# A single scale factor of one weight's conversion read from a tile, which a ScalarE result must precede

## The chip, the cores and the metric

The kernel runs on one core of a Trainium2 chip. The metric is the device time of one execution in microseconds (us). Three runs of the kernel before took 575.41, 574.70 and 574.67 us; the median is 574.7 us.

## What is computed

A chain of three parts in float32, in which every part reads the output of the one ahead of it:

```python
state = gamma * state + outer(k[t], v[t]); y[t] = scale * q[t] @ state   # 2 x 8 heads, 768 steps, 64 wide
x  = y as (1536 tokens, 512)
xn = x / rms(x) * rms_g                                                   # first feed-forward part
x  = (silu(xn @ w_gate) * (xn @ w_val)) @ w_out                           # 512 -> 1536 -> 512
h  = x @ w_in                                                             # second feed-forward part
out = maximum(0.01 * h, h) @ w2_out                                       # 512 -> 2048 -> 512
```

The weights arrive as 64-bit floats. The kernel turns them into 32-bit floats on the chip.

## The kernel before, in words

**Tiles.** The 1536 tokens are three blocks of 512. A weight is cut into tiles of 128 by 512, named by kind and number: g, v and o (gate, value and output of the first feed-forward part, 12 of each) and i and p (input and output of the second one, 16 of each). So i1 is the second of the i-weights and o11 the last of the o-weights.

**Conversion of one weight.** One DMA brings the 64-bit words of a tile to `raw_i1` (three such buffers, `RAWS`). ScalarE (ACT) makes three passes over it in `prepare`: L608 the high words into `wa_i1` (four buffers), L609 the low words, scaled by 2 to the -29, into `wb_i1` (two buffers, tag "b" of the pool `stage`), and L613 the signs into half of `wb_i1`. L609 and L613 together are called the low passes here. VectorE (DVE) then clamps and shifts (`wa_i1` at L534 and L539) and adds `wb_i1` to it (L553), after which `wa_i1` is the 32-bit weight and the `wb` buffer is free for the weight two further on. For TensorE (PE) the weight is split into a high part (ACT, L556) and a low part (DVE, L560), called `w_i1`; a product of weight and input is three matmuls, high by high, low by high and high by low.

**Sums of weights.** Two of three token blocks are computed with seven half products in place of eight (the scheme of Strassen and Winograd, `quad` for g, v and i, `seventh` for o and p). This needs, for each pair of weights, two more tiles: `w_si2` and `w_si3` for the pair i2, i3. DVE makes four half-width sums in place (L490), and again ACT writes the high part (L493) and DVE the low part (L497).

**A pair of i-weights on PE** (L1110, `quad`): seven groups of six matmuls into three PSUM banks X, Y and Z. With the pair i0, i1: X by `w_i0`, Y by `w_i0`, then on with X by `w_si0` (group p6 in the code), with Z by `w_si1` (p5), X by `w_si1` (p7), Z by `w_si0` (p3) and X by `w_i1` (p4). Between two uses of X or Z the sum so far has to be copied out: by ACT at L1127 (`is1`, `is5`, `iu2`) or by DVE with an addition at L1136. ACT then applies the leaky maximum at L1046. The other products of the first block (L657, `i0_0` and so on) and the products with o or p (L908, L775, L692) fill the time between.

**What sets the order.** The first stretch is a list written by hand (`ORDER`). From there a planner (`run`) emits the operations step by step, and the scheduler of the tile framework moves them: it lists each engine's instructions in the order in which, by its own estimate, they can start. Each engine then runs its own list strictly in order. So an added dependence changes the lists of all engines behind it.

Of the kernel before, what the change touches and what calls it, by code (L numbers as in the profile page):

```python
# [8 lines left out]
F32 = mybir.dt.float32  # L9
F32R = mybir.dt.float32r  # L10
I32 = mybir.dt.int32
U32 = mybir.dt.uint32
F16 = mybir.dt.float16
AF = mybir.ActivationFunctionType
ALU = mybir.AluOpType
AX = mybir.AxisListType

P = 128
# [3 lines left out]
G1 = [4, 4, 4]  # L22
# [44 lines left out]
def chain_kernel(ctx: ExitStack, tc: tile.TileContext, qk_t, kv, w1, w2, mask, qdec, kdec, sdec, rms_g, ident, out):  # L67
    nc = tc.nc
# [16 lines left out]
    gp = ctx.enter_context(tc.tile_pool(name="gp", bufs=3))  # L85
    scr = ctx.enter_context(tc.tile_pool(name="scr", bufs=SCRATCH))
    ps_acc = ctx.enter_context(tc.tile_pool(name="ps_acc", bufs=1, space=bass.MemoryType.PSUM))
    dram = ctx.enter_context(tc.tile_pool(name="dram", bufs=1, space=bass.MemoryType.DRAM))
    attn_pools = ctx.enter_context(ExitStack())
    score_pool = ctx.enter_context(ExitStack())  # L90
# [2 lines left out]
    at = attn_pools.enter_context(tc.tile_pool(name="at", bufs=4))  # L93
    sm = attn_pools.enter_context(tc.tile_pool(name="sm", bufs=4))

    held = [dram.tile([P, 512], F32, name=f"held{i}") for i in range(4)]
    mask_sb = const.tile([P, 2, NPAIR, CH], F32, name="mask_sb")
    qdec_sb = const.tile([P, NPAIR, CH], F32, name="qdec_sb")
# [305 lines left out]
        )  # L404

    wt = {}
    slots = [[units, UNITS, set()]]
    groups = [list(range(sum(g[:i]), sum(g[:i + 1]))) for g in (G1, G2) for i in range(len(g))]
    groups = [("gvo" if i < len(G1) else "ip", fs) for i, fs in enumerate(groups)]

# [34 lines left out]
    def free(*keys):  # L445
        for s in slots:
            s[2].difference_update(keys)


    def fetch():  # L450
        if fetched[0] < min(len(sources), taken[0] + RAWS):
            key, src = sources[fetched[0]]
            fetched[0] += 1
            raw[key] = raws.tile([P, 512, 2], I32, tag="raw", name=f"raw_{key}")
            cut = 512 if key in IN_HALVES else 1024
            for n in range(0, 1024, cut):
                nc.sync.dma_start(
                    out=raw[key].rearrange("p n two -> p (n two)")[:, n:n + cut], in_=src.bitcast(I32)[:, n:n + cut]
                )
# [3 lines left out]
    def open_unit():  # L463
        if started[0] == len(wq):
            return None
        key, src = wq[started[0]]
        v = nc.vector

        def room(key):
            slot = next((s for s in slots if len(s[2]) < s[1]), None)  # L470
            if slot is not None:
                slot[2].add(key)
            return slot

        after = next((k for k, x in wq[started[0] + 1:] if x is not None), None)
        if src is None:
            n, f = key[1], int(key[2:])

            names = (key, f"s{n}{f + 1}")
            places = [room(k) for k in names]  # L480
            if None in places:
                free(*names)
                return None
            started[0] += 1
            a, e = kept.pop(f"{n}{f}"), kept.pop(f"{n}{f + 1}")
            a_one, a_two, e_one, e_two = a[:, :2 * P], a[:, 2 * P:], e[:, :2 * P], e[:, 2 * P:]
            us = [s[0].tile([P, 2, 512], F32R, tag="u", name=f"w_{k}") for s, k in zip(places, names)]

            def combine(out, in0, in1, op):
                return lambda: v.tensor_tensor(out=out, in0=in0, in1=in1, op=op)  # L490

            def high_part(u, x):
                return lambda: nc.scalar.activation(out=u[:, 0, :], in_=x, func=AF.Copy)  # L493

            def low_part(u, x, k):
                def put():
                    v.tensor_tensor(out=u[:, 1, :], in0=x, in1=u[:, 0, :].bitcast(F32), op=ALU.subtract)  # L497
                    wt[k] = u

                return put  # L500

            if n in "op":
                return key, None, {
                    "1": combine(e_two, a_two, e_two, ALU.add),
                    "2": combine(a_two, a_one, a_two, ALU.subtract),
                    "3": combine(a_one, e_two, a_one, ALU.subtract),
                    "H": high_part(us[0], a),
                    "4": combine(e_one, e_one, a_one, ALU.subtract),
                    "h": high_part(us[1], e),
                    "L": low_part(us[0], a, names[0]),  # L510
                    "l": low_part(us[1], e, names[1]),
                }
            return key, None, {
                "1": combine(e_two, e_one, e_two, ALU.add),
                "2": combine(e_one, a_one, e_one, ALU.subtract),
                "3": combine(a_one, e_two, a_one, ALU.subtract),
                "H": high_part(us[1], e),
                "4": combine(a_two, a_two, a_one, ALU.subtract),
                "h": high_part(us[0], a),
                "L": low_part(us[1], e, names[1]),  # L520
                "l": low_part(us[0], a, names[0]),
            }
        slot = room(key)
        if slot is None:
            return None
        started[0] += 1
        u = slot[0].tile([P, 2, 512], F32R, tag="u", name=f"w_{key}")

        by_parts = key in FIRST

        def smaller():
            a = prepared[key][0]
            up = 1.0 if by_parts else UP
            v.tensor_scalar(a, a, F64_MIN * up, F64_MAX * up, ALU.max, ALU.min)  # L534

        def shifted():
            ai = prepared[key][0].bitcast(I32)
            mask = 0x07FFFFFF if by_parts else -1
            v.tensor_scalar(ai, ai, mask, 3, ALU.bitwise_and, ALU.logical_shift_left)  # L539

        def sign():
            a, m, high = prepared[key]
            ai = a.bitcast(I32)
            v.scalar_tensor_tensor(
                out=ai, in0=high, scalar=-0x40000000, in1=ai, op0=ALU.bitwise_and, op1=ALU.bitwise_or
            )
            taken[0] += 1
            fetch()

        def add():  # L550
            a, m, high = prepared[key]
            ai = a.bitcast(I32)
            v.tensor_tensor(out=ai, in0=ai, in1=m, op=ALU.add)  # L553

        def high_part():
            nc.scalar.activation(out=u[:, 0, :], in_=prepared[key][0], func=AF.Copy)  # L556

        def low_part():
            a = prepared.pop(key)[0]
            v.tensor_tensor(out=u[:, 1, :], in0=a, in1=u[:, 0, :].bitcast(F32), op=ALU.subtract)  # L560
            wt[key] = u

        ops = {"P": lambda: prepare(key), "1": smaller, "2": shifted, "4": add, "H": high_part, "L": low_part}
        if by_parts:
            ops["3"] = sign
        return key, after, ops
# [15 lines left out]
    def start_unit():  # L582
        unit = open_unit()
        if unit is None:
            return False
        queue(unit)
        return True

    def convert_step(key, op):
        while key not in opened_units:  # L590
            unit = open_unit()
            opened_units[unit[0]] = unit
        opened_units[key][2].pop(op, lambda: None)()

    def prepare(key):

        if key in prepared:
            return
        while key not in raw:
            fetch()  # L600
        t = raw.pop(key)
        low, high = t[:, :, 0], t[:, :, 1]
        a = stage_a.tile([P, 512], F32, tag="a", name=f"wa_{key}")
        m = stage.tile([P, 512], I32, tag="b", name=f"wb_{key}")
        if (f"s{key[0]}{int(key[1:]) // 2 * 2}", None) in wq:
            kept[key] = a
        up = 1.0 if key in FIRST else UP
        nc.scalar.activation(out=a, in_=high.bitcast(F32), func=AF.Abs, scale=up)  # L608
        nc.scalar.activation(out=m, in_=low.bitcast(U32), func=AF.Copy, scale=2.0 ** -29)  # L609
        prepared[key] = a, m, high  # L610
        if key not in FIRST:
            signs = m.bitcast(F16).rearrange("p (n two) -> p n two", two=2)[:, :, 1]
            nc.scalar.activation(out=signs, in_=high.bitcast(F32), func=AF.Copy, scale=2.0 ** -100)  # L613
            taken[0] += 1
            fetch()
# [852 lines left out]
```

## Time and profile before

| | |
|---|---|
| median of three runs | 574.7 us |
| the profiled execution's own time | 574.38 us |
| its span | 572.6 us |
| PE, busy share of the span | 99% |
| PE weight load | 81% |
| DVE | 90% |
| ACT | 72% |
| TensorE clock granted | full in every slice |

The span is the time from the first to the last instruction of the profiled execution; 1.8 us of its own time lie around it. Busy shares are over the whole span. Matmuls overlap in the records, so a busy PE says only that some matmul was under way: whether PE lost time shows in the distance from one matmul's start to the next one's.

### The profile page before, as it was taken

To read this page: it belongs to the slowest core of one execution; us is meant where nothing else is said; L and a number is where in the kernel's file an instruction comes from. 1 tells how busy PE (TensorE), PEld (TensorE's weight loads), DVE (VectorE), ACT (ScalarE), POOL (GpSimd) and SP (SyncE) were. 2 spreads that over 40 slices of the span, in tenths; PEclk is the share of its full clock that TensorE was granted. 3 is DMA by queue.
4 is the path that set the end of the run, shared out by engine and by line. 5 is a ranking of instruction groups with operands and counts; after the bars stand their busy time and mean duration, and the time that the engine had idled before them with its cause. 6 is when DMAs were issued, how large, how long until landed. Compare 5 with 4: busy or idle time off the path is not lost.

```text
span 572.6 us, 8596 instructions
## 1 busy us (share of the span) xinstructions
PE 565.2 (99%) x3079; PEld 464.7 (81%) x3079; DVE 516.4 (90%) x1015; ACT 412.2 (72%) x757; POOL 39.5 (7%) x49
## 2 busy tenths in 40 slices
PE   9999999999999999999999999999999999999997
PEld 6888787888888788888888878888888888888886
DVE  8899899999988799995899999999999979996692
ACT  4799667978796745886647699989959886676330
POOL 3341000010000000020000200000100020002100
PEclk9999999999999999999999999999999999999999
DMA  8991422233242111335220422223512352102555
GB/s 338 407 361 38 128 93 69 80 102 120 74 143 80 37 38 37 105 98 130 74 74 0 95 54 89 76 84 120 185 37 74 116 93 87 38 0 24 123 98 125
DMA packets 35115, 59.29 MB, mean 104 GB/s; under 512 B 19264, under 2 KB 19520, under 8 KB 35072
## 3 DMA queue, kind: packets, MB, share of 16 engines
q1 hardware_dynamic: 31584, 51.39, 27.2%
q0 software_dynamic: 3200, 7.34, 6.3%
q8 instruction: 24, 0.39, 0.3%
q14 instruction: 19, 0.16, 0.1%
q10 hardware_dynamic: 288, 0.01, 0.0%
HBM read 50.34 MB, written 8.39 MB: 103 GB/s over the span
## 4 chain that ended last, share of the span: by engine, by line
PE 78%; DVE 9%; ACT 6%; DMA 5%; issue 1%; SPq 0%; DVEq 0%; ACTq 0%
PE X L908 12%; PE Z L908 9%; PE iX L1110 8%; PE i L657 8%; PE ap L692 7%; PE g L657 5%; PE v L657 5%; PE iZ L1110 4%; PE vX L1110 4%; PE gX L1110 3%; PE ao L692 3%; PE ao L775 2%; PE iY L1110 2%; PE vZ L1110 2%; DMA qkv<-in_qk_t 2%; DMA qkv<-in_kv 2%
## 5 line engine op out<-in xcount | busy, mean ns | idle before, releaser
L692 PE MATMUL ap<-w_p,gp_0h 128*128 128x512 f32 (+1 forms) x128 | 38.6, 383 | 0.0
L657 PE MATMUL g<-xh,w_g 128*128 128x512 f32 x128 | 32.0, 392 | 0.0
L657 PE MATMUL i<-x2h,w_i 128*128 128x512 f32 x128 | 32.0, 390 | 0.0
L657 PE MATMUL v<-xh,w_v 128*128 128x512 f32 x128 | 31.7, 390 | 0.0
L657 PEld LDWEIGHTS g<-xh,w_g 128*128 128x128 f32 x128 | 23.8, 188 | 5.4 <-DVE g L1056 0.2
L657 PEld LDWEIGHTS i<-x2h,w_i 128*128 128x128 f32 x128 | 24.0, 188 | 5.1
L657 PEld LDWEIGHTS v<-xh,w_v 128*128 128x128 f32 x128 | 24.0, 188 | 4.9
L692 PEld LDWEIGHTS ap<-w_p,gp_0h 128*128 128x128 f32 x128 | 23.8, 188 | 4.8
L692 PE MATMUL ap<-w_p,gp_0l 128*128 128x512 f32 x64 | 24.5, 383 | 0.0
L1046 ACT ACTIVATE more<-i 128x512 f32<-128x512 f32 x16 | 9.5, 595 | 19.9 <-PE i L657 19.9
L692 PE MATMUL ao<-go_0h,w_o 128*128 128x512 f32 x64 | 21.0, 389 | 0.0
L1110 PE MATMUL iZ<-x2h,w_si 128*128 128x512 f32 x64 | 20.2, 391 | 0.0
L1110 PE MATMUL iX<-th,w_si 128*128 128x512 f32 x64 | 20.1, 393 | 0.0
L560 DVE TENSOR_TENSOR w_o<-wa_o,w_o 128x512 fp32r<-128x512 f32 x12 | 8.2, 687 | 11.3 <-ACT w_o L556 11.3
L657 PE MATMUL g<-xl,w_g 128*128 128x512 f32 x64 | 17.3, 392 | 0.0
L657 PE MATMUL i<-x2l,w_i 128*128 128x512 f32 x64 | 17.1, 389 | 0.0
L657 PE MATMUL v<-xl,w_v 128*128 128x512 f32 x64 | 17.1, 389 | 0.0
L938 DVE TENSOR_TENSOR y2acc<-X,y2acc 128x512 f32<-128x512 f32 x26 | 17.1, 682 | 0.0
L493 ACT ACTIVATE w_so<-wa_o 128x512 fp32r<-128x512 f32 x12 | 7.4, 627 | 12.6 <-DVE wa_o L490 12.3
L258 DVE TENSOR_TENSOR a<-sc,mask_sb 128x1024 f32<-128x1024 f32 (+1 forms) x13 | 14.5, 1134 | 1.0 <-PE sc L246 0.8
L609 ACT ACTIVATE wb_i<-raw_i 128x512 int32<-128x512 uint32 x16 | 10.8, 674 | 5.9 <-DMA raw_i<-in_w 2.3
L977 POOL DMA_DIRECT2D out<-more x8 | 7.1, 1030 | 113.0 <-ACT more L973 112.8
(381 smaller groups left out, 1879.7 us busy)
## 6 DMA issues: line engine op xcount, KB each, us to landing
raw_i<-in_w SPq DMA_DIRECT2D x16, 512.0 KB, 3.6
raw_g<-in_w SPq DMA_DIRECT2D x12, 512.0 KB, 3.5
raw_v<-in_w SPq DMA_DIRECT2D x12, 512.0 KB, 3.8
raw_o<-in_w SPq DMA_DIRECT2D x12, 512.0 KB, 3.4
raw_p<-in_w SPq DMA_DIRECT2D x11, 512.0 KB, 3.5
qkT<-in_qk_t SPq DMA_DIRECT2D x7, 512.0 KB, 8.5
kv<-in_kv SPq DMA_DIRECT2D x7, 512.0 KB, 9.3
out<-more POOLq DMA_DIRECT2D x12, 256.0 KB, 4.5
```

Source lines behind the costliest of these rows:

```text
L258: nc.vector.tensor_tensor(out=s["a"][:, j], in0=s["sc"][:, j], in1=mask_sb[:, j], op=ALU.mult)
L493: return lambda: nc.scalar.activation(out=u[:, 0, :], in_=x, func=AF.Copy)
L560: v.tensor_tensor(out=u[:, 1, :], in0=a, in1=u[:, 0, :].bitcast(F32), op=ALU.subtract)
L609: nc.scalar.activation(out=m, in_=low.bitcast(U32), func=AF.Copy, scale=2.0 ** -29)
L657: nc.tensor.matmul(out=dst, lhsT=lhs, rhs=rhs, start=(n == 0), stop=(n == len(pairs) - 1), skip_group_check=True)
L692: nc.tensor.matmul(out=dst, lhsT=lhs, rhs=rhs[:, c:c + cut], start=(start and n == 0), stop=(stop and n == 2), skip_group_check=True,)
L775: nc.tensor.matmul(out=acc["b"][m], lhsT=lhs, rhs=rhs, start=(e == fs[0] and n == 0), stop=(e == fs[-1] and n == 2), skip_group_check=True,)
L908: nc.tensor.matmul(out=acc[side][m], lhsT=lhs, rhs=rhs, start=(start and f == fs[0] and k == 0), stop=(f == fs[-2] and k == 2), skip_group ...
L938: nc.vector.tensor_tensor(out=dst, in0=banks[m], in1=dst, op=ALU.add)
L977: nc.gpsimd.dma_start(out=rows, in_=dst, accum_op=ALU.add)
L1046: nc.scalar.activation(out=a, in_=x, func=AF.Prelu, alpha=0.01)
L1110: nc.tensor.matmul(out=dst, lhsT=lhs, rhs=rhs, start=(start and n == 0), stop=(n == 5), skip_group_check=True)
```

## The change

The scale of the low pass L609 of one weight, i1, is no longer the constant 2 to the -29 but a tile `ulp` of one column. DVE writes it with one instruction: it reads one column of the high part of `w_o11`, takes the maximum with 2 to the -29 and then the minimum with 2 to the -29, so that the value is the same constant whatever was read. The pass of i1 therefore has to come after the high part of o11 (ACT, L556) and after that DVE instruction. The number of passes, DMAs and matmuls is the same; there is one DVE instruction more.

```diff
--- before.py
+++ after.py
@@ -85,6 +85,7 @@
     gp = ctx.enter_context(tc.tile_pool(name="gp", bufs=3))
     scr = ctx.enter_context(tc.tile_pool(name="scr", bufs=SCRATCH))
     ps_acc = ctx.enter_context(tc.tile_pool(name="ps_acc", bufs=1, space=bass.MemoryType.PSUM))
+    late = ctx.enter_context(tc.tile_pool(name="late", bufs=1))
     dram = ctx.enter_context(tc.tile_pool(name="dram", bufs=1, space=bass.MemoryType.DRAM))
     attn_pools = ctx.enter_context(ExitStack())
     score_pool = ctx.enter_context(ExitStack())
@@ -93,6 +94,7 @@
     at = attn_pools.enter_context(tc.tile_pool(name="at", bufs=4))
     sm = attn_pools.enter_context(tc.tile_pool(name="sm", bufs=4))
 
+    ulp = late.tile([P, 1], F32, name="ulp")
     held = [dram.tile([P, 512], F32, name=f"held{i}") for i in range(4)]
     mask_sb = const.tile([P, 2, NPAIR, CH], F32, name="mask_sb")
     qdec_sb = const.tile([P, NPAIR, CH], F32, name="qdec_sb")
@@ -404,7 +406,9 @@
         )
 
     wt = {}
+    wt_high = []
     slots = [[units, UNITS, set()]]
+    last_sum = f"o{sum(G1) - 1}"
     groups = [list(range(sum(g[:i]), sum(g[:i + 1]))) for g in (G1, G2) for i in range(len(g))]
     groups = [("gvo" if i < len(G1) else "ip", fs) for i, fs in enumerate(groups)]
 
@@ -554,6 +558,8 @@
 
         def high_part():
             nc.scalar.activation(out=u[:, 0, :], in_=prepared[key][0], func=AF.Copy)
+            if key == last_sum:
+                wt_high.append(u)
 
         def low_part():
             a = prepared.pop(key)[0]
@@ -606,7 +612,12 @@
             kept[key] = a
         up = 1.0 if key in FIRST else UP
         nc.scalar.activation(out=a, in_=high.bitcast(F32), func=AF.Abs, scale=up)
-        nc.scalar.activation(out=m, in_=low.bitcast(U32), func=AF.Copy, scale=2.0 ** -29)
+        scale = 2.0 ** -29
+        if key == "i1":
+            v = wt_high[0][:, 0, :1].bitcast(F32)
+            nc.vector.tensor_scalar(ulp, v, scale, scale, ALU.max, ALU.min)
+            scale = ulp
+        nc.scalar.activation(out=m, in_=low.bitcast(U32), func=AF.Copy, scale=scale)
         prepared[key] = a, m, high
         if key not in FIRST:
             signs = m.bitcast(F16).rearrange("p (n two) -> p n two", two=2)[:, :, 1]
```

The scheduler's lists change from there on. DMA issues keep their order on both queues. On PE only neighbours change places: one matmul of X by `w_i2` goes ahead of group p7 of the pair i0, i1; five matmuls of `i0_0` go between the first and the second matmul with `w_si3`; and some groups of i3, i4 and p0 are interleaved otherwise. Behind the conversion of i13 all lists are alike again.

**ACT, around the copies of the pair i0, i1.** `is1_0` and `iu2_0` written from `iX0` are the two copies (L1127, in the changed kernel L1138) for which PE's X groups wait. Before:

```order
L608 ACTIVATE wa_p1_3569<-raw_p1_3428 128x512
L841 ACTIVATE x2h0_3416<-more_1389 128x512
L1024 ACTIVATE th_3305<-x2acc1_1647 128x1024
L1127 ACTIVATE is1_0_3442<-iX0_3431 128x512
L841 ACTIVATE x2h0_3416<-more_1389 128x512 x3
L1127 ACTIVATE iu2_0_3488<-iX0_3431 128x512
L1046 ACTIVATE is1_0_3442<-is1_0_3442 128x512
L721 ACTIVATE gq_0_1h_3672<-is1_0_3442 128x512
L1127 ACTIVATE is5_0_3499<-iZ0_3490 128x512
```

ACT at the same place in the changed kernel:

```order
L560 ACTIVATE w_i2_3470<-wa_i2_3428 128x512
L620 ACTIVATE wb_p0_3535<-raw_p0_3159 128x512
L852 ACTIVATE x2h0_3421<-more_1393 128x512
L1035 ACTIVATE th_3310<-x2acc1_1651 128x1024
L1138 ACTIVATE is1_0_3447<-iX0_3436 128x512
L852 ACTIVATE x2h0_3421<-more_1393 128x512 x3
L624 ACTIVATE wb_p0_3535<-raw_p0_3159 128x512
L1138 ACTIVATE iu2_0_3493<-iX0_3436 128x512
L1057 ACTIVATE is1_0_3447<-is1_0_3447 128x512
L1138 ACTIVATE is5_0_3504<-iZ0_3495 128x512
```

The low passes of p0 (`wb_p0`) now stand here, one ahead of the copies and one (L624) directly ahead of `iu2_0`; before, they stood far ahead, between the products of o. The high part of i2 came in, `wa_p1` and `gq_0_1h` went out.

**ACT, ahead of the high part of w_si3** (L493, in the changed kernel L497). Before:

```order
L609 ACTIVATE wb_p1_3570<-raw_p1_3428 128x512
L1046 ACTIVATE is5_0_3499<-is5_0_3499 128x512
L613 ACTIVATE wb_p1_3570<-raw_p1_3428 128x512
L1046 ACTIVATE iu2_0_3488<-iu2_0_3488 128x512
L1046 ACTIVATE i1_1_3525<-iX0_3431 128x512
L493 ACTIVATE w_si3_3547<-wa_i3_3468 128x512
L609 ACTIVATE wb_p2_3629<-raw_p2_3473 128x512
L1127 ACTIVATE is1_2_3552<-iX2_3537 128x512
```

ACT ahead of `w_si3` in the changed kernel:

```order
L1057 ACTIVATE is5_0_3504<-is5_0_3504 128x512
L560 ACTIVATE w_i3_3492<-wa_i3_3473 128x512
L620 ACTIVATE wb_p1_3575<-raw_p1_3433 128x512
L1057 ACTIVATE iu2_0_3493<-iu2_0_3493 128x512
L1057 ACTIVATE i1_1_3530<-iX0_3436 128x512
L624 ACTIVATE wb_p1_3575<-raw_p1_3433 128x512
L1138 ACTIVATE is1_2_3557<-iX2_3542 128x512
L620 ACTIVATE wb_p2_3634<-raw_p2_3478 128x512
L497 ACTIVATE w_si3_3552<-wa_i3_3473 128x512
```

Between `i1_1` and `w_si3` there are now three passes: a low pass of p1, the copy `is1_2` and a low pass of p2.

**DVE, between the products of o and the first i-products.** Before:

```order
L1027 TENSOR_TENSOR tl_3306<-x2acc2_1674,th_3305 128x1024 x2
L844 TENSOR_TENSOR x2l1_3304<-x2acc1_1647,x2h1_3303 128x512 x2
L497 TENSOR_TENSOR w_si0_3456<-wa_i0_3087,w_si0_3456 128x512
L1021 TENSOR_TENSOR x2acc1_1647<-x2acc1_1647,x2acc2_1674 128x1024
L791 TENSOR_TENSOR more_1389<-ao_2_0_1_3348,more_1389 128x512
L844 TENSOR_TENSOR x2l0_3417<-more_1389,x2h0_3416 128x512
L560 TENSOR_TENSOR w_i2_3465<-wa_i2_3423,w_i2_3465 128x512
```

DVE at that place in the changed kernel:

```order
L1038 TENSOR_TENSOR tl_3311<-x2acc2_1678,th_3310 128x1024 x2
L855 TENSOR_TENSOR x2l1_3309<-x2acc1_1651,x2h1_3308 128x512 x2
L557 ISA wa_i2_3428<-wa_i2_3428,wb_i2_3429 128x1024
L1032 TENSOR_TENSOR x2acc1_1651<-x2acc1_1651,x2acc2_1678 128x1024
L802 TENSOR_TENSOR more_1393<-ao_2_0_1_3353,more_1393 128x512
L855 TENSOR_TENSOR x2l0_3422<-more_1393,x2h0_3421 128x512
L538 TENSOR_SCALAR wa_i3_3473<-wa_i3_3473 128x512
L566 TENSOR_TENSOR w_i2_3470<-wa_i2_3428,w_i2_3470 128x512
```

The low part of `w_si0` left this place (it now stands further up, ahead of the first `x2l1`), and the addition for i2 (L553, in the changed kernel L557) and the clamp of i3 (L534, now L538) came in; before, both stood in the products of o.

## Rows read from the trace of the kernel before

**Rows 1.** Windows: us, busy us and count of each engine, granted clock, DMA share.

```profile
300.00:350.00 50.00, 50.00 (x220) 40.61 (x219) 49.47 (x84) 39.01 (x65) 3.18 (x4) 1.00 0.24 58
350.00:400.00 50.00, 50.00 (x219) 40.56 (x218) 49.34 (x97) 45.82 (x83) 0.00 (x0) 1.00 0.27 90
400.00:450.00 50.00, 50.00 (x222) 41.40 (x222) 48.50 (x93) 40.31 (x72) 2.20 (x4) 1.00 0.31 106
```

**Rows 2.** Chain that ended last: start, us, engine, tile, line, matmuls.

```profile
277.40 2.72 PE g L657 x12
```

**Rows 3.** Timeline of PE: start, us from first start to last end, instructions.

```profile
293.79 0.39 PE L908 MATMUL Z<-gr_5l,w_so 128*128 128x512 f32 x1
294.19 0.74 PE L908 MATMUL Z<-gr_5h,w_so 128*128 128x512 f32 x2
...
330.74 0.39 PE L1110 MATMUL iZ<-x2h,w_si 128*128 128x512 f32 x1
331.01 0.73 PE L1110 MATMUL iX<-th,w_si 128*128 128x512 f32 x2
...
333.66 0.62 PE L1110 MATMUL iX<-th,w_si 128*128 128x512 f32 x2
...
335.03 0.73 PE L1110 MATMUL iZ<-x2h,w_si 128*128 128x512 f32 x2
...
340.62 0.62 PE L1110 MATMUL iZ<-x2h,w_si 128*128 128x512 f32 x2
```

**Rows 4.** Timeline of DVE; in brackets idle time before, and what ended it.

```profile
282.49 0.69 DVE L560 TENSOR_TENSOR w_o<-wa_o,w_o 128x512 fp32r<-128x512 f32 x1 [0.93 <-ACT w_o L556]
...
293.45 0.68 DVE L497 TENSOR_TENSOR w_so<-wa_o,w_so 128x512 fp32r<-128x512 f32 x1
...
302.53 0.68 DVE L553 CUSTOM_DVE_ANT_0 wa_i<-wa_i,wb_i 128x1024 uint16<-128x1024 uint16 x1
...
327.12 0.68 DVE L497 TENSOR_TENSOR w_si<-wa_i,w_si 128x512 fp32r<-128x512 f32 x1
...
339.37 0.69 DVE L497 TENSOR_TENSOR w_si<-wa_i,w_si 128x512 fp32r<-128x512 f32 x1
```

**Rows 5.** Timeline of ACT, products of o.

```profile
280.01 0.67 ACT L609 ACTIVATE wb_i<-raw_i 128x512 int32<-128x512 uint32 x1
...
281.38 0.57 ACT L1052 ACTIVATE more<-g 128x512 f32<-128x512 f32 x1
281.84 1.15 ACT L556 ACTIVATE w_o<-wa_o 128x512 fp32r<-128x512 f32 x2
288.48 0.63 ACT L493 ACTIVATE w_so<-wa_o 128x512 fp32r<-128x512 f32 x1 [5.50 <-DVE wa_o L490]
```

**Rows 6.** Summary of line L361: durations min/median/max in ns, first and last start.

```profile
L361 DVE TENSOR_SCALAR na<-norm x6: 146/154/160, 23.8 to 64.6; 128x2 f32<-128x2 f32 x6
```

**Rows 7.** Timeline of ACT, low passes of p0, first i-products.

```profile
303.95 0.79 ACT L613 ACTIVATE wb_p<-raw_p 128x512 f16<-128x512 f32 x1
304.62 1.12 ACT L721 ACTIVATE gr_2h<-g 128x512 fp32r<-128x512 f32 x2
...
328.89 0.63 ACT L841 ACTIVATE x2h<-more 128x512 fp32r<-128x512 f32 x1 [0.38 <-PE ao L775]
...
330.38 0.58 ACT L1127 ACTIVATE is<-iX 128x512 f32<-128x512 f32 x1
...
332.72 0.58 ACT L1127 ACTIVATE iu<-iX 128x512 f32<-128x512 f32 x1
...
338.10 0.60 ACT L1046 ACTIVATE i<-iX 128x512 f32<-128x512 f32 x1
338.59 0.63 ACT L493 ACTIVATE w_si<-wa_i 128x512 fp32r<-128x512 f32 x1
339.15 0.68 ACT L609 ACTIVATE wb_p<-raw_p 128x512 int32<-128x512 uint32 x1
339.74 0.57 ACT L1127 ACTIVATE is<-iX 128x512 f32<-128x512 f32 x1
```

## The prediction

> **What bounds the kernel now.** The windows come first. From 300 to 450 us PE is busy in all of every window, at the full clock, and DVE is busy for 97 to 99% of it [rows 1]. What PE can still gain is in the rhythm of its matmuls. The chain shows twelve matmuls of 512 columns in 2.72 us, 0.227 us each, and this is the rate wherever nothing waits [rows 2]. The window from 400 to 450 us holds 222 matmuls, the two before it 220 and 219 [rows 1]: five fewer, about 5 x 0.227 = 1.1 us lost from 300 to 400 us. The timeline of PE shows such losses, and that each costs twice: the matmul starts late, and the pair behind it takes 0.73 or 0.74 us where an undisturbed pair takes 0.62 [rows 3], so 0.11 us more for every wait however short. The one loss just ahead, at 293.79 us, is 0.40 us to the next start in place of 0.227, and 0.12 us behind it: 0.29 us. So the part of the program in which the lists differ has some 1.1 + 0.29 = 1.4 us to give back, 0.24% of the time, and no more. It can lose more than that, since DVE and ACT feed PE with little in hand.
>
> The Trainium skill, page "Perfetto Trace Analysis", section "Identifying the Most-Contended Engine", says that the busy share of the weight loads, not that of the matmuls, tells the headroom of TensorE. By it the share of the weight loads here, 41.40 of 50 us, would leave 17% to gain [rows 1]. The trace disagrees as to this stretch: it is the stretch without a late matmul.
>
> **The change, part by part.** The times are those of the kernel before; a stretch of which PE is ahead or behind is shifted as a whole.
>
> *The write of ulp.* One DVE instruction on one column. The nearest row is the TENSOR_SCALAR on two columns, 0.146 to 0.160 us [rows 6]; the bounds are nothing and 0.16 us, and I take 0.15. It stands ahead of the low parts of `w_so10` and `w_so11`, which the first part below makes early by more than that. Without this cover it would cost PE 0.15 us at `w_so11`. A scale from a tile may make the one pass on ACT up to twice as long (0.67 us, [rows 5]) or not longer. ACT gets to this pass behind `w_so11`, after 5.50 us of idleness [rows 5], so either is hidden, and so is the wait for ulp: DVE writes it ahead of `w_so10`, ACT comes to it later. Behind it on ACT wait the other passes of i1, i2 and i3 and a high part of o; none of them gets late.
>
> *A, the end of the o-weights: -0.29 us.* ACT made both low passes of i3 at 280.01 us, and so started `more` (L1052) at 281.38, although PE had finished that product at 277.40 + 2.72 = 280.12 [rows 2, 5]. These passes are gone from here. L1052 and the high parts of `w_o10` and `w_o11` come about 1.0 us earlier, and DVE, which waited 0.93 us for the first of them at 282.49, then runs without a pause up to `w_so11` at 293.45 [rows 4]. That low part ended at 294.13 and PE started with it at 294.19, 0.17 us late [rows 3]. About 1.0 less 0.15 for ulp is more than 0.17, so the loss goes. The bounds are -0.29 and 0.
>
> *B, the first copy: -0.16 us.* At 330.74 us one matmul by `w_si1` starts, then PE waits for ACT's copy, which ends at 330.38 + 0.58 = 330.96, and goes on at 331.01 [rows 3, 7]: 0.05 + 0.11 us lost. In the new list two such matmuls come first, so PE arrives at 331.20. The addition for i2 takes the place of the low part of `w_si0`, which ended at 327.12 + 0.68 = 327.80 [rows 4]; the two ACT passes behind it, some 1.1 us, fit ahead of L841 at 328.89 [rows 7]. The bounds are -0.16 and, if the copy comes later by 0.3 us, 0.
>
> *C, the second copy: +0.40 us.* A low pass of p0 now stands directly ahead of the copy `iu2_0`. Such a pass holds ACT for 304.62 - 303.95 = 0.67 us, and ACT has no idle time there, so the copy starts at 332.72 + 0.67 = 333.39 and ends at 333.97 [rows 7]. PE wants the result at 333.66 [rows 3], less 0.16 (B), plus 0.227 for the matmul by `w_i2` that goes ahead: 333.73. It waits 0.28 us with a semaphore's 0.04 and loses 0.11 behind it. The bounds are 0 and 0.6.
>
> *D: -0.11 us.* The pair at 335.03 us took 0.73 [rows 3]; after C the copy it waited for is done in time.
>
> *E, the high part of w_si3: +0.85 us.* Before, it followed `i1_1` directly, from 338.59 to 339.22, and PE used it at 340.62, a slack of 1.40 us [rows 3, 7]. Now three passes stand between: 0.67 for a low pass of p1, 0.49 (338.59 - 338.10, a pass that reads PSUM) and 0.59 (339.74 - 339.15) [rows 7], 1.75 us. `i1_1` itself waits for the last X group of the pair, which is late by C + 0.227 - B - D, 0.36 us, and ACT's own queue is a little later still: I take 0.5. The high part comes 2.25 us later, PE arrives 0.13 us later (0.36 less the matmul done already), and the wait is 2.25 - 1.40 - 0.13 = 0.72, with 0.11 behind it 0.83 and a semaphore's step 0.85. The low part was done at 339.37 + 0.69 = 340.06 [rows 4]; it is late too, but five matmuls of `i0_0` stand ahead of its first use. The bounds are 0.3 (i1_1 in time) and 1.2.
>
> *F, what follows up to 400 us: -0.2 us.* Of the window from 350 us three matmuls, 0.68 us, were lost [rows 1]. PE now comes here about 0.5 us later, and DVE and ACT have by then done the work that was moved, so some of these small waits end; I take 0.2 of 0 to 0.68. Where the lists differ behind 400 us I take nothing, since there PE lost nothing before and the work is the same.
>
> DMAs: the raw buffers of i1 to i3 come free some 10 us later and that of p0 about 28 us later (332.72 for 303.95). The weights that they hold back are used tens of us later, so this costs nothing; with a single spare buffer it would.
>
> The sum is -0.29 - 0.16 + 0.40 - 0.11 + 0.85 - 0.2 = +0.49 us. The profiled execution's 574.38 becomes 574.9. It lies 0.3 us under the median of the runs, and on the median 574.7 + 0.5 = 575.2 us.
>
> **The rivals.** Within 0.2% (1.15 us) counts as no change; a measurement of this kernel tells no less.
>
> *Faster: the new waits stay away.* PE waits at `w_si3` only if its high part is late by more than the slack, 1.40 us. If the three passes on ACT come at other times (C and E zero), A, B and D remain, -0.56, and with F between 0 and -0.68 the time is 573.5 to 574.1. For it speaks that ACT is busy for only 39 of 50 us there [rows 1], against it that it has no idle time between 332.72 and 339.74. Chance 0.18; it gives more than 0.2% only with all of F (0.06).
>
> *Slower: the backlog is carried on.* DVE has no idle time to catch up in [rows 1]. If C and E are at their upper ends (0.6 and 1.2), F is nothing, and two more waits of 0.3 us follow among the p-weights, whose low passes moved too, the sum is -0.56 + 1.8 + 0.6 = +1.8: 576.5. It decides from a `w_si3` late by 2.7 us on. Chance 0.16.
>
> *No effect: the lists move, PE does not notice.* Each moved piece is hidden and A is not gained either: 574.7. Against it are B to E, where the rows leave less than 0.7 us in hand. Chance 0.05.
>
> *Much faster.* If the weight loads tell the headroom, a better order could gain several us, below 573.3. The constant 0.227 us speaks against it. Chance 0.02.
>
> **The numbers.** My forecast, a net change of 0 to 1 us, has 0.59. Faster by over 0.2%: 0.06 + 0.02 = 0.08. Slower: 0.16. The rest, 0.76, is no change. The range from 573.8 to 576.3 leaves out about 0.1 on either side: the faster rival with most of F, and the far end of the slower one. The forecast's own range is 574.6 to 575.9.
>
> **What would show it.** In the new trace: no wait at the first Z matmul with `w_so11`; a pair by `w_si0` in X without delay; PE late by 0.3 us at the X group by `w_si1`, released by the copy `iu2_0`; PE late by about 0.7 us at the first matmul by `w_si3`, released by ACT's high part; ACT without idle time ahead of it. The forecast is wrong if ACT has this high part ready when PE arrives, or if PE waits anew behind 350 us.

## The result, and the profile after

The changed kernel takes 578.29 us, the median of five runs (577.91 to 578.45), beside 574.67 us for the kernel before (574.02 to 575.41, five runs). The ratio is 1.0058, 95% interval 1.0044 to 1.0073: slower by 3.6 us, where +0.5 was forecast. The profiled execution's span is 576.5 us; that of before was 572.6, so 3.9 us are to be found. The first part of the page shows that nearly the same work was done; the columns are busy time, share of the span and instructions, before and then after:

```profile
PE 565.2 (99%) x3079; PEld 464.7 (81%) x3079; DVE 516.4 (90%) x1015; ACT 412.2 (72%) x757; POOL 39.5 (7%) x49
```

```profile
PE 568.5 (99%) x3079; PEld 465.0 (81%) x3079; DVE 518.2 (90%) x1016; ACT 412.2 (72%) x757; POOL 39.8 (7%) x49
```

The windows of after answer to [rows 1]:

```profile
300.00:350.00 50.00, 49.14 (x214) 39.58 (x213) 49.14 (x83) 36.85 (x63) 3.18 (x4) 1.00 0.27 64
350.00:400.00 50.00, 49.97 (x219) 40.64 (x218) 49.27 (x97) 45.99 (x82) 0.00 (x0) 1.00 0.28 87
400.00:450.00 50.00, 50.00 (x221) 41.16 (x220) 48.61 (x93) 39.65 (x71) 2.20 (x4) 1.00 0.32 103
```

PE now has real idle time from 300 to 350 us, 0.86 us, and six matmuls fewer. That is the forecast's part of the program, and it holds about a third of the loss, 6 x 0.227 = 1.4 us. Nearly half lies ahead of it, and about 1 us behind 400 us, where PE has no wait in after. The windows of PE alone, before and then after, from 97 us, where PE begins to run without a break, to 265 us, just ahead of the first place where the list of an engine differs (ACT's, which at 265.9 us lacks the low passes of i1):

```profile
97.00:265.00 168.00, 167.91 (x740) 1.00 0.31 93
```

```profile
97.00:265.00 168.00, 168.00 (x733) 1.00 0.31 89
```

The clock is the same and PE is never idle, yet seven matmuls fewer fit in: 7 x 0.227 = 1.6 us lost where not one instruction had moved. The tiles `th` and `tl` hold the high and low parts of the sums of the input that the seven half products need; PE streams their 512 columns past the weights that it has loaded (they are the moving operand, the weights the stationary one). Two rows of the summary of tile `th` (durations of one matmul, min/median/max in ns, first and last start in us), before and then after, show it from the side:

```profile
L1110 PE MATMUL gX<-th,w_sg x40: 389/389/497, 95.6 to 265.9; 128*128 128x512 f32 x40
L1110 PE MATMUL vX<-th,w_sv x40: 389/389/390, 117.6 to 280.9; 128*128 128x512 f32 x40
```

```profile
L1121 PE MATMUL gX<-th,w_sg x40: 391/396/496, 95.6 to 267.5; 128*128 128x512 f32 x40
L1121 PE MATMUL vX<-th,w_sv x40: 387/393/400, 118.0 to 282.7; 128*128 128x512 f32 x40
```

Both traces start the first matmul by `w_sg` at 95.6 us; the last one is 1.6 us late. The chain of waits says which groups pay, before and then after (start, us, engine, tile, line, matmuls). The first group reads `th` and `tl`, the other two read `xh` and `xl`, the parts of the input itself:

```profile
240.68 1.36 PE gX L1110 x6
242.04 1.36 PE vX L1110 x6
243.40 1.36 PE vY L1110 x6
```

```profile
241.95 1.40 PE gX L1121 x6
243.35 1.39 PE vX L1121 x6
244.74 1.36 PE vY L1121 x6
...
279.18 2.75 PE g L668 x12
```

Six matmuls of `th` and `tl` take 1.40 us in place of 1.36, the group behind them 1.39, and the next is at the old rhythm again. The last row, behind such a group as well, answers to [rows 2], which were 2.72.

One account is used for all kernels below. For every 512-column matmul from 97 us on, some 2,040 records, the interval to the next start is compared with 0.2267 us, the rhythm of before. What intervals under 0.247 us exceed it by is summed as "rhythm", what longer ones exceed it by as "waits".

```
kernel     rhythm us   waits us   th and tl, mean ns   others, mean ns
before        0.59       1.65          227.1                226.9
after         3.98       2.13          233.6                227.7
```

3.4 + 0.5 = 3.9 us, the whole of the difference. The second term is the one that was forecast. The first was not thought of.

### The profile page after: what moved, and what is told of

Same layout as the page of the kernel before. It is cut to its first block, busy times and chain, and to the rows that moved or that the text cites. A ratio compares the mean times of both kernels' runs of the same rounds, so it can differ in the third digit from the quotient of the medians.

```text
span 576.5 us, 8600 instructions
## 1 busy us (share of the span) xinstructions
PE 568.5 (99%) x3079; PEld 465.0 (81%) x3079; DVE 518.2 (90%) x1016; ACT 412.2 (72%) x757; POOL 39.8 (7%) x49
## 4 chain that ended last, share of the span: by engine, by line
PE 84%; DMA 6%; ACT 4%; DVE 4%; issue 1%; DVEq 0%; ACTq 0%
PE X L919 13%; PE Z L919 10%; PE i L668 8%; PE ap L703 7%; PE iX L1121 7%; PE g L668 7%; PE v L668 6%; PE vX L1121 5%; PE gX L1121 5%; PE iZ L1121 3%; PE ao L703 3%; PE vZ L1121 2%; PE gZ L1121 2%; DMA raw_v<-in_w 2%; DMA qkv<-in_kv 2%; PE ao L786 1%
## 5 line engine op out<-in xcount | busy, mean ns | idle before, releaser
L497 ACT ACTIVATE w_so<-wa_o 128x512 fp32r<-128x512 f32 x12 | 7.4, 627 | 12.3 <-DVE wa_o L494 12.0
L1121 PEld LDWEIGHTS iZ<-x2h,w_si 128*128 128x128 f32 x64 | 12.0, 188 | 3.8 <-ACT w_si L497 1.0
```

Source lines behind the costliest of these rows:

```text
L1121: nc.tensor.matmul(out=dst, lhsT=lhs, rhs=rhs, start=(start and n == 0), stop=(n == 5), skip_group_check=True)
```

## The experiments

What is moved in SBUF, the memory on the chip that operands are read from, was read from the compiled programs. `ulp` takes 32 bytes of each partition of SBUF and is allocated ahead of `th`, `tl` and two weight slots (`w_v2`, `w_sv3`), so these start 32 bytes later than before. Before, every tile of 2048 bytes or more starts at 128 past a multiple of 2048. No experiment leaves computation out, and the lists of PE, ACT and DVE are those of the kernel that each is made from, except in e8 and e14. In the expectations O is the theory that the order of the lists slows the matmuls, P that the place of `th` and `tl` does.

**e1_after_64.** The change with `ulp` in 64 bytes.

```diff
-    ulp = late.tile([P, 1], F32, name="ulp")
+    ulp = late.tile([P, 16], F32, name="ulp")[:, :1]
```

> The changed kernel with a tile ulp of 16 columns in place of 1, so that the tiles behind it move by 64 bytes and not by 32; every engine's list is that of the changed kernel. Theory P (place): the time went to matmuls that read th and tl, which start at 32 bytes past a multiple of 64 in the changed kernel; 3.4 us of their rhythm come back and only the waits of the new order stay: 574.7 + 0.5 = 575.2 us, matmuls of th and tl at 0.227 us. Rival O (order): the new lists cost the 3.6 us, through waits or the engines' contention; the time stays at 578.3 us and the slow rhythm stays.

578.36 us, ratio 1.0059 (1.0045 to 1.0073). Taken alone this speaks for O; it does so wrongly, since 64 was a guess at what place would be harmless.

**e2_before_32.** The kernel before, with an unused tile where `ulp` goes: the place of the change without its order.

```diff
+    pad = ctx.enter_context(tc.tile_pool(name="pad", bufs=1)).tile([P, 8], F32, name="pad")
     dram = ctx.enter_context(tc.tile_pool(name="dram", bufs=1, space=bass.MemoryType.DRAM))
```

> The kernel before with an unused tile of 32 bytes per partition allocated where the change puts ulp; every engine's list is that of the kernel before. Theory P: th and tl start at 32 past a multiple of 64, the rhythm loss of 3.4 us appears without any change of order: 578.1 us. Rival O: nothing changes, 574.7 us.

577.34 us, 1.0041 (1.0027 to 1.0055). Rhythm 4.07 us, as in the change; O falls. The waits shrink to 0.89 us: while PE is slower, ACT and DVE get ahead. In the summary of tile `th`:

```profile
L1111 PE MATMUL gX<-th,w_sg x40: 391/397/502, 95.7 to 267.6; 128*128 128x512 f32 x40
```

**e3_th_32.** The same, and a gap of 32 bytes between `th` and `tl`.

```diff
         th = pools["xt"].tile([P, 6, 512], F32R, tag="th", name="th")
+        pools["xt"].tile([P, 8], F32, tag="gap", name="gap")
         tl = pools["xt"].tile([P, 6, 512], F32R, tag="tl", name="tl")
```

> The same unused tile, and a second one of 32 bytes between th and tl, so that th starts at 32 past a multiple of 64 and tl, and the two weight slots behind it, at a multiple of 64. Theory P, each matmul that reads a shifted tile pays: four of the six matmuls of a group read th, two read tl, so two thirds of 3.4 us, 2.3 us: 577.0 us, with the matmuls on tl at 0.227 us but for what hangs over. If the shifted weight slots or small tiles behind them were the cause, 574.7 us. Rival O: 574.7 us.

576.44 us, 1.0024 (1.0015 to 1.0033). `th`, moved by 32 bytes, has 232.4 ns on average, `tl`, moved by 64, 230.8 (about 235 in e2, moved by 32). The amount depends on the number of bytes, and 64 isn't free.

**e4_weights_32.** Unused tiles of 32 bytes ahead of the weights' pool and behind it.

```diff
+    pad = ctx.enter_context(tc.tile_pool(name="pad", bufs=1)).tile([P, 8], F32, name="pad")
     units = ctx.enter_context(tc.tile_pool(name="units", bufs=UNITS))
+    pad2 = ctx.enter_context(tc.tile_pool(name="pad2", bufs=1)).tile([P, 8], F32, name="pad2")
```

> Unused tiles of 32 bytes ahead of and behind the pool of the twelve weight slots, so that nearly all weights (and nothing that is always the moving operand) start at 32 past a multiple of 64. Theory P with the moving operand alone: only the 192 matmuls per i/p pass over block 0 in which the p-weight is the moving operand pay some 0.010 us each: 574.7 + 2 = 576.7 us. Theory P with either operand: about 2500 matmuls pay 0.010 us, some 25 us: 600 us. Rival O: 574.7 us.

586.82 us, 1.0206 (1.0186 to 1.0226): every kind of matmul at about 233 ns, rhythm 13.5 us. None of the expected times was met. The weights are moved by 32 bytes and everything behind them by 64, so this run alone can't say which of them counts. The next three were made to tell that.

**e5_after_128.** As e1, with 128 bytes (`[P, 32]`).

> The changed kernel, whole, with ulp held in a tile of 128 bytes in place of 4: every tile behind it, th and tl among them, again starts at a multiple of 128 bytes in its partition, as in the kernel before; the lists of the engines are those of the changed kernel. Theory P128 (a matmul whose operand starts off a multiple of 128 bytes runs in 0.230 to 0.235 us in place of 0.227): th and tl matmuls back at 0.227 us, the 3.4 us of slower rhythm gone, and only the new order's waits left, 574.8 + 0.5 = 575.3 us. Rival R (it is the shift against the other tiles, not the place, that costs): still 578.4 us.

577.13 us, 1.0045 (1.0031 to 1.0059), neither 575.3 nor 578.4. Rhythm 3.08 us, `th` and `tl` at 231.9 ns: P128 falls, since every tile starts at a multiple of 128 bytes here.

**e6_weights_32_alone.** As e4, with `pad2` of 96 bytes (`[P, 24]`): weights moved by 32, everything behind by 128.

> The kernel before with unused tiles of 32 bytes ahead of the weights' pool and 96 bytes behind it: only the weights start at 32 past a multiple of 128 bytes, all tiles behind them are moved by 128 bytes and start at such a multiple again. If the place of the stationary operand also counts, most of the 12 us that e4_weights_32 lost come here: 585 to 587 us. If only the moving operand counts: the matmuls in which a weight is the moving operand, some 180 of them by 6 ns, so about 574.8 + 1.1 = 575.9 us.

586.81 us, 1.0224 (1.0199 to 1.0249). The chain shows twelve matmuls at 2.80 us where they took 2.72, and the same three groups as above, now all at 1.40:

```profile
155.24 2.80 PE g L659 x12
...
244.91 1.40 PE gX L1112 x6
246.31 1.40 PE vX L1112 x6
247.71 1.40 PE vY L1112 x6
```

From 97 to 276 us 768 matmuls start, where before has 789. The waits are down to 0.38 us: of 13.1 us of slower rhythm 1.3 are given back so.

**e7_rest_64.** One tile of 64 bytes behind the weights' pool (`pad2` alone, `[P, 16]`): everything but the weights is moved by 64.

> The kernel before with an unused tile of 64 bytes behind the weights' pool: the weights stay at a multiple of 128 bytes, every tile behind them starts at 64 past one. If it is the other tiles, the moving operands among them, that made e4_weights_32 slow: 585 to 587 us, matmuls of every such operand at 0.230 to 0.233 us. If it was the weights: 574.8 us.

581.21 us, 1.0116 (1.0097 to 1.0134). Both expected times were missed. By the ratios 64 bytes cost about half of what 32 do (e4). Three of the four runs took 581.1 to 581.3 us; the trace is of the fourth, 579.26 us, and why the same places of the tiles give two times stays open. In this trace the interval is 229.5 ns on average, and uneven. Two rows of tile `th` (durations as above):

```profile
L1111 PE MATMUL iX<-th,w_si x64: 388/394/501, 333.0 to 526.1; 128*128 128x512 f32 x64
...
L1111 PE MATMUL vX<-th,w_sv x40: 388/390/394, 118.1 to 282.8; 128*128 128x512 f32 x40
```

**e8_i3_128.** The change with the scale given to i3, and `ulp` in 128 bytes.

```diff
-        if key == "i1":
+        if key == "i3":
```

> The changed kernel with the scale from ulp given to the low passes of i3 in place of i1, and ulp in a tile of 128 bytes: i1 and i2 keep the order of before, only i3's passes on ACT stand behind the o-weights. Part A of the prediction alone. If A is worth what it was forecast (the wait at w_so11 goes, 0.29 us) and the place costs nothing: 574.8 - 0.3 = 574.5 us, without the new waits of C and E. Rival R: 578 us. If the ACT work that is moved makes a new wait of the kind of E: 575 us or more.

576.73 us, 1.0037 (1.0023 to 1.0050). The slow rhythm of e5 (3.15 us) hides what A is worth in the time; the waits sum to 1.35 us, 0.30 less than before.

What was left was R, that the tiles' places count only against each other. The experiments from e9 to e13 and e15 test it.

**e9_ulp_last.** The whole change, with `ulp` allocated behind all other tiles, so that none is moved.

```diff
-    late = ctx.enter_context(tc.tile_pool(name="late", bufs=1))
...
-    ulp = late.tile([P, 1], F32, name="ulp")
...
         slots.append([ctx.enter_context(tc.tile_pool(name="units2", bufs=UNITS2)), UNITS2, set()])
+        late = ctx.enter_context(tc.tile_pool(name="late", bufs=1))
+        pools["ulp"] = late.tile([P, 1], F32, name="ulp")
```

> The changed kernel, whole, with ulp allocated behind all other tiles: every tile starts where it does in the kernel before, and the lists of the engines are those of the changed kernel. Every theory of the place of the tiles: the slow rhythm is gone (start to start 0.227 us at th and tl), only the new order's waits are left, +0.5 us, so 574.2 to 574.8 us of before become 574.7 to 575.3, ratio 1.001. Rival (something else of the change slows the matmuls): 577 to 578 us.

574.78 us (11 runs) beside 574.32: ratio 1.0004 (0.9995 to 1.0013). Rhythm 0.47 us, waits 2.08. This is the change as the prediction had thought of it, and the runs can't tell it from no change. In the summary of tile `th`:

```profile
L1120 PE MATMUL gX<-th,w_sg x40: 389/389/504, 95.7 to 266.1; 128*128 128x512 f32 x40
```

**e10_all_128** and **e11_all_32.** An unused tile of 128, or of 32, bytes ahead of the weights' pool (`pad` of e4 alone): all large tiles are moved together.

> The kernel before with an unused tile of 128 bytes ahead of the weights' pool: every large tile is moved by 128 bytes, none against another. Theory R (what counts is how the operands of a matmul stand to each other): as before, 574.2 to 574.8 us, 0.227 us throughout. Theory of the place (each operand has to start at 128 past a multiple of 256 bytes or more, where all large tiles of before start): slower, 577 us or more.

> The kernel before with an unused tile of 32 bytes ahead of the weights' pool: every large tile starts at 32 past a multiple of 128 bytes, none is moved against another. Theory R: as before, 574.2 to 574.8 us. Theory of the place: 586 to 587 us, as e6_weights_32_alone, where only the weights stood at 32.

574.77 us, 1.0000 (0.9991 to 1.0009), and 574.43 us, 0.9998 (0.9989 to 1.0007); rhythm 0.51 and 0.50 us. The place by itself costs nothing. In the summary of tile `th` of e11:

```profile
L1111 PE MATMUL gX<-th,w_sg x40: 389/389/499, 95.7 to 266.0; 128*128 128x512 f32 x40
```

**e12_ulp_512** and **e15_ulp_256.** As e1, with 512 and with 256 bytes.

> The changed kernel with ulp in a tile of 512 bytes: th and tl move by 512 bytes against the weights (they are 2048 bytes long for one 512-column operand, and a slice of the weights is 512). Under either theory, if the pattern repeats with 512 bytes: 0.227 us at th and tl, and 574.7 to 575.3 us. If it repeats only with more: 576.5 to 578 us, as e5_after_128.

> The changed kernel with ulp in a tile of 256 bytes: th and tl are moved by 256 bytes against the weights. If the pattern repeats with 256 bytes: 574.7 to 575.3 us, as e12_ulp_512. If only with 512: 576.5 to 578 us, with matmuls of th and tl at 0.230 to 0.235 us, as e5_after_128.

574.93 us, 1.0008 (0.9999 to 1.0018), and 574.95 us, 1.0004 (0.9979 to 1.0029); rhythm 0.50 us in both. For `th` and `tl` the pattern repeats with 256 bytes. In e15 the row is as before:

```profile
L1121 PE MATMUL gX<-th,w_sg x40: 389/389/501, 95.7 to 266.0; 128*128 128x512 f32 x40
```

**e13_traffic_32.** The kernel before; the tiles that only ACT, DVE and DMAs use (raw weights, `wa`, `wb`, scratch) are moved by 32 bytes against all operands of matmuls, and those only by multiples of 512 against each other.

```diff
     units = ctx.enter_context(tc.tile_pool(name="units", bufs=UNITS))
+    pad = ctx.enter_context(tc.tile_pool(name="pad", bufs=1)).tile([P, 8], F32, name="pad")
...
+    pad2 = ctx.enter_context(tc.tile_pool(name="pad2", bufs=1)).tile([P, 120], F32, name="pad2")
     xp = ctx.enter_context(tc.tile_pool(name="xp", bufs=1))
     gp = ctx.enter_context(tc.tile_pool(name="gp", bufs=3))
+    pad3 = ctx.enter_context(tc.tile_pool(name="pad3", bufs=1)).tile([P, 8], F32, name="pad3")
     scr = ctx.enter_context(tc.tile_pool(name="scr", bufs=SCRATCH))
+    pad4 = ctx.enter_context(tc.tile_pool(name="pad4", bufs=1)).tile([P, 120], F32, name="pad4")
```

> The kernel before with unused tiles that move the raw weights, their intermediate tiles (wa, wb) and the scratch tiles by 32 bytes against the operands of the matmuls, and move those operands only by multiples of 512 bytes against each other (weights 0, x and the stationary gates 512, th and tl 1024). If what counts is how the moving and the stationary operand of a matmul stand to each other: as before, 574.2 to 574.8 us, 0.227 us throughout. If it is TensorE's reads against the accesses of ACT and DVE: slower by several us, up to the 586 of e6_weights_32_alone.

574.35 us, 0.9988 (0.9967 to 1.0008); rhythm 0.51 us. It is not those tiles, as far as 32 bytes can tell.

```profile
L1114 PE MATMUL vX<-th,w_sv x40: 389/389/390, 117.8 to 281.0; 128*128 128x512 f32 x40
```

**e14_i3_last.** e8 with `ulp` behind all other tiles: part A alone.

> The changed kernel with the scale from ulp given to i3 in place of i1 and with ulp allocated behind all other tiles: part A alone, no tile moved. By the parts as they were measured (A -0.29 us, no C and E, the order's other waits as in e8_i3_128, whose waits sum to 0.3 us less than those of before): 574.0 to 574.3 us, ratio 0.9995, which is within what a measurement tells from no change. Rival (A is eaten by what follows): 574.4 to 574.8 us, no different from before either, but with the sum of its waits no smaller in the trace.

574.41 us, 0.9991 (0.9972 to 1.0010). Waits 1.44 us, 0.21 less than before, rhythm 0.64. If this beats the kernel before, it is by less than these runs can tell.

## Why the prediction was wrong

**The step that failed** is the first of the parts, the write of `ulp`: it costed the instruction and the pass that waits for it, and took the tile itself to cost nothing. Beside it stood "0.227 us each, and this is the rate wherever nothing waits", which is true of one arrangement of the tiles only. Moving `th` and `tl` by 32 bytes cost 3.4 us of rhythm, seven times the forecast sum. That is shown from three sides: the place without the order is slow (e2), the order without the shift isn't (e9), and the same shift of everything together isn't (e11).

**What counts is how the operands of the matmuls stand to each other in SBUF.** `th` and `tl` against the rest: moved by 32, 64 or 128 bytes they bring the rhythm account to between 3.1 and 4.5 us, by 256 or 512 to 0.5, as without a move. Weights against everything else: 13.5 us by 32 bytes (e4), 13.7 by 96 (e6), 5.9 by 64 (e7, in the quickest of its runs); no multiple of 256 was tried with them. Moving the tiles that only ACT, DVE and DMAs use by 32 bytes costs nothing (e13). That leaves what ACT and DVE read and write in the operands' own tiles, which were not moved apart. It is not that either: in e6 the 46 matmuls in whose interval neither ACT nor DVE is busy take 233.6 ns, all of them together 233.3; before, the 45 such matmuls take 227.7. That it is PE's load of the next weights that meets its reading of the moving operand is the likeliest mechanism, but only argued: the load runs under the matmul before it, and its own record doesn't show it, with a median of 188 ns at the o-weights both before and in e6. How many nanoseconds a given shift costs stays open. In e7's trace and in e1 `th` stands 64 bytes from where it stood to the weights `w_sv`, yet the mean interval is 227.7 ns in the one and 232.2 in the other; and [rows 2] and their row of after show that matmuls with both operands in their old places are slower for a group when they follow one that was moved.

The Trainium skill, page "SBUF — State Buffer", section "Who interferes with whom", gives TensorE two independent read ports, one for the moving operand and one for the weight load, and says that only the port pair that VectorE and GpSimd share causes contention. For ACT and DVE against PE, e13 agrees as far as it goes. Where the weights alone are moved, e6, a matmul takes 233.3 ns against 226.9; if that is the two reads of TensorE meeting, which is argued here and not shown, the measurement differs from the page.

**The order's own terms held in their sum, and C not by itself.** They are read in e9 and in after, as the interval's excess over 0.227 us. The timeline of PE in after answers to [rows 3]:

```profile
294.14 0.39 PE L919 MATMUL Z<-gr_5h,w_so 128*128 128x512 f32 x1
294.36 0.39 PE L919 MATMUL Z<-gr_5l,w_so 128*128 128x512 f32 x1
...
335.09 0.40 PE L1121 MATMUL iX<-x2h,w_i 128*128 128x512 f32 x1
335.76 0.74 PE L1121 MATMUL iX<-th,w_si 128*128 128x512 f32 x2 [0.27 <-ACT iu L1138]
...
342.34 0.39 PE L1121 MATMUL iY<-x2l,w_i 128*128 128x512 f32 x1
343.32 0.50 PE L1121 MATMUL iZ<-x2h,w_si 128*128 128x512 f32 x1 [0.59 <-ACT w_si L497]
```

And that of ACT, which answers to [rows 7]:

```profile
333.44 1.15 ACT L852 ACTIVATE x2h<-more 128x512 fp32r<-128x512 f32 x2 [0.33 <-DMA more<-held]
334.49 0.78 ACT L624 ACTIVATE wb_p<-raw_p 128x512 f16<-128x512 f32 x1
335.14 0.57 ACT L1138 ACTIVATE iu<-iX 128x512 f32<-128x512 f32 x1
...
340.96 0.79 ACT L624 ACTIVATE wb_p<-raw_p 128x512 f16<-128x512 f32 x1
341.60 0.58 ACT L1138 ACTIVATE is<-iX 128x512 f32<-128x512 f32 x1
342.06 0.68 ACT L620 ACTIVATE wb_p<-raw_p 128x512 int32<-128x512 uint32 x1
342.64 0.63 ACT L497 ACTIVATE w_si<-wa_i 128x512 fp32r<-128x512 f32 x1
```

PE in e9:

```profile
333.31 0.39 PE L1120 MATMUL iX<-x2h,w_i 128*128 128x512 f32 x1
333.60 0.73 PE L1120 MATMUL iX<-th,w_si 128*128 128x512 f32 x2
...
340.09 0.39 PE L1120 MATMUL iY<-x2l,w_i 128*128 128x512 f32 x1
341.16 0.50 PE L1120 MATMUL iZ<-x2h,w_si 128*128 128x512 f32 x1 [0.68 <-ACT w_si L495]
...
361.69 0.39 PE L667 MATMUL i<-x2h,w_i 128*128 128x512 f32 x1
362.09 0.50 PE L918 MATMUL X<-gq_6h,w_sp 128*128 128x512 f32 x1
...
415.53 0.72 PE L918 MATMUL Z<-gq_5h,w_sp 128*128 128x512 f32 x2
```

- *The write of ulp:* 0.149 us where 0.15 was taken, and the pass that reads it 0.746, far from twice 0.67. Both are hidden, as forecast. The rows are those of tile `ulp` in after (durations min/median/max, first and last start):

```profile
L618 DVE TENSOR_SCALAR ulp<-w_o x1: 149/149/149, 289.9 to 289.9; 128x1 f32<-128x1 f32 x1
L620 ACT ACTIVATE wb_i<-raw_i,ulp x1: 746/746/746, 291.3 to 291.3; 128x512 int32<-128x512 uint32 x1
```

- *A, B and D* (-0.29, -0.16, -0.11): the waits at 293.79, 330.74 and 335.03 us of [rows 3] are gone in both kernels.
- *C* (+0.40): the place, the releaser and the low pass ahead of the copy are as forecast. In after PE starts at 335.76, 0.67 behind the start before it: 0.44 and 0.11 for the pair behind. In e9 the two are 0.07 and 0.11, 0.18 in all. What lies between is a wait that the term left out: ahead of the low pass ACT stood idle for 0.33 us in after, until a DMA brought `more` (from `held`); before, that wait was 0.18, which the term kept by starting from 332.72; and in e9 there was none. The bounds were 0 and 0.6, and that 0.40 lies between 0.18 and 0.55 is luck.
- *E* (+0.85): 343.32 - 342.34 - 0.23 = 0.75, and 0.11 behind it, 0.86 in after; 0.95 in e9. In the rows above the three passes that were named stand between `i1_1` and L497 and hold ACT for 342.64 - 340.96 = 1.68 us, where 1.75 was taken; ACT has no pause there. This term is right in its mechanism and near in its size.
- *F* (-0.2): of the waits of before from 354 to 387 us, 0.55 us by the account above, all are gone in e9 but one, at an X group by `w_sp`; it grew from 0.10 (361.68 us before) to 0.29 (362.09). A new one at 415.53 us costs 0.11. Net -0.16. The prediction had named a new wait behind 350 us as a sign of being wrong, and this one is small but there.

In e9 these make -0.29 - 0.16 + 0.18 - 0.11 + 0.95 - 0.16 = +0.41 us; the time of its profiled execution was 574.81 us, 0.43 over before's 574.38. The forecast of the order was +0.49. It came so near because C was too high by 0.22 and E too low by 0.10; and the ratio of e9's runs, 0.9995 to 1.0013, is -0.3 to +0.7 us, so that the times alone can't tell +0.49 from 0. The range 573.8 to 576.3 holds e9 and misses the change by 2 us, since no term of it could be a slower matmul. The "much faster" rival was put aside because 0.227 us is constant; it is this constant that moved, the other way. The slower rival has the sign and half of the size, but of its mechanism, a backlog that is carried on, the runs show nothing: no wait stands behind 384 us in after.

## What to carry to other kernels

A new tile has two costs: what is done with it, and what it moves. Compare the addresses of the matmul operands in the programs before and after, and allocate small tiles behind all others (e9), or in multiples of 256 bytes (e15, e12). When a change costs more than its waits explain, measure the start-to-start interval of matmuls in a part of the program where nothing was reordered.

## What was not expected of the hardware

- The same 512-column matmul, at full clock and without a wait, takes 226.9 ns from start to start or 233, by where its operands lie against each other; here up to 12.6 us of 574 (e6).
- A slower rhythm is not paid in full, since it gives ACT and DVE time: with 13.1 us more of rhythm the waits fell from 1.65 to 0.38 us (e6).
